# Transposes of batch 0's remainder and of half of batch 1 moved from TensorE to DMA, with new slots and a new order of loads

## The chip, the cores and the metric

One core of one Trainium2 chip. The metric is device microseconds of one execution; a kernel's figure is the median of several executions. Small comparisons are made as ratios: the mean time of one kernel's fast runs over that of the other's in the same rounds, with a 95% interval, so a ratio is not quite the quotient of the two medians quoted beside it.

Two more numbers are used. The profiled span is that of one traced execution. "The touched stretch" is, within one trace, the time from the first down-projection matmul (about 26 us) to the first up-projection matmul of the second token tile (83 us before).

## The reference

A retention layer (linear attention with decay) feeds a mixture of four experts, all of them applied to every token:

```python
# q, k, v: (8 batches, 8 heads, 576 positions, 64)
scores = q @ k^T / sqrt(64)
ret    = scores * gamma_h ** (i - j)   # i >= j, else 0
x      = (ret @ v), heads side by side           # (4608 tokens, 512)
out    = sum_e p[:, e] * (relu(x @ w1[e]) @ w2[e])   # w1: 512x1024, w2: 1024x512, e = 0..3
```

The kernel computes in bf16 with fp32 accumulation. It takes the tokens in nine tiles of 512; the attention of later batches is woven in between the expert matmuls of earlier tiles.

## The kernel before

The first tile is special: the weights are still on their way, and batch 1 is computed from four "units" (two halves of the sequence by two groups of heads), each with its own loads. The last 64 positions of a batch are its "remainder". Work is put into numbered slots: slot n is run after the n-th group of expert matmuls, and every engine executes its own part of the program in that order.

```python
# k and q have to be transposed before the scores. By TensorE, through PSUM and an ACT copy:
def trans_pe(self, between=0):                       # of a unit
    self.qk = atp.tile([128, 2, 2, 2, C], BF16, tag="qkT", name="qkT0")
    pt = ring_tile("pt", [128, 2, 2, 2, 2 * C], BF16)     # PSUM ring, 4 tiles
    for i, n in ((1, "k"), (0, "q")):
        ...
        nc.tensor.transpose(pt[:, i, r, g, 0:C], ..., ident)
    nc.scalar.activation(self.qk[...], pt[...], Copy)

# ... or by DMA:
def trans_dma(self):
    self.qk = atp.tile([128, 2, 2, 2, C], BF16, tag="qkT", name="qkT1")
    for i, n in ((1, "k"), (0, "q")):
        nc.sync.dma_start_transpose(out=self.qk[:, i]..., in_=self.bf(n)...)

# one group of an expert's up-projection (slots 0-3, 8-11, 16-19, 24-27)
def up_group(h, t, e, i):
    ph = ring_tile("ph", [128, 2, NT])
    ...                                              # 8 matmuls, 1.73 us
    if t == 0:
        nc.scalar.activation(h[:, fk:fk + 2, :], ph, Relu)   # frees the PSUM tile
        return

# loads, all in GpSimd's queue, in this order
load_w1(2); load_w2(2); load_v(0); load_v(1); load_w1(3); load_v(2); load_w2(3)   # load_v(3) later

def v_cast(u):
    vs[u].cast("k", nc.vector); vs[u].cast("q", nc.vector)
    vs[u].cast("v", nc.scalar)                       # ACT, in program order
    if u > 1:
        vs[u].trans_dma()                            # units 2 and 3 only
    if u == 0:
        load_v(3)

remainder(slots, 0, (-1, 13, 15, 16, 17))            # load, cast, transposes (TensorE), scores, values
for u, (c, tr, sc, o) in enumerate(((17, 20, 22, 23), (19, 22, 24, 25), (24, 0, 28, 29), (25, 0, 29, 30))):
    ...                                              # cast, transpose, scores and kv, values of unit u
```

So before, TensorE transposes the remainder of batch 0 and units 0 and 1; DMA transposes units 2 and 3, at a time when the loads are over.

Of the kernel before, what the change touches and what calls it, by code (L numbers as in the profile page):

```python
# [10 lines left out]
BF16 = mybir.dt.bfloat16  # L11
Copy = mybir.ActivationFunctionType.Copy
# [11 lines left out]
def kernel(  # L24
# [10 lines left out]
    nc = tc.nc  # L35
    B, H, S, D = q.shape
    N, E = moe_domain_probs.shape
# [3 lines left out]
    C = 128  # L41
    NC = 4
    SM = NC * C
    R = S - SM
    NP = H // 2
# [13 lines left out]
    atp = ctx.enter_context(tc.tile_pool(name="atp", bufs=2))  # L59
    ppool = ctx.enter_context(tc.tile_pool(name="ppool", bufs=4))  # L60
# [5 lines left out]
    def ring_tile(name, shape, dt=FP32):  # L66
        return ring.tile(shape, dt, tag="ring", name=name)
# [5 lines left out]
    def load_pair(t, b, p, eng=nc.sync):  # L73
        for n, src in srcs:
            for j in range(2):
                eng.dma_start(out=t[n][:, :, j, :],
                              in_=src[b, 2 * p + j, 0:SM, :].rearrange("(c p) d -> p c d", p=C))

    def load_rem(b, eng=nc.sync):
        for j in range(2):  # L80
            for n, src in (("k", k), ("v", v)):
                eng.dma_start(out=rawr[n][64 * j:64 * j + 64, :, j, :],
                                  in_=src[b, j:H:2, SM:S, :].rearrange("g t d -> t g d"))
        eng.dma_start(out=rawr["q"][0:R, :, :, :].rearrange("t g j d -> t (g j) d"),
                          in_=q[b, :, SM:S, :].rearrange("h t d -> t h d"))

    rawr = {n: const.tile([128, NP, 2, D], FP32, name=f"rawr_{n}") for n, _ in srcs}
    bfr = {n: const.tile([128, NP, 2, D], BF16, name=f"bfr_{n}") for n, _ in srcs}
    raw1 = {n: const.tile([128, NC, 2, D], FP32, name=f"raw1_{n}") for n, _ in srcs}
# [9 lines left out]
    def load_w1(e, f=slice(0, F)):  # L99
        return nc.gpsimd.dma_start(out=w1_sb[e][:, :, f], in_=moe_w1[e][:, f].rearrange("(dc p) f -> p dc f", p=128))  # L100

    def load_w2(e):
        return nc.gpsimd.dma_start(
            out=wx[e // 2][:, (e % 2) * NFC:(e % 2 + 1) * NFC, :, :].rearrange("p a b c -> p a (b c)"),
            in_=moe_w2[e].rearrange("(fc p) d -> p fc d", p=128))
# [9 lines left out]
    def load_unit(raw, b, hf, g, eng):  # L115
        for n, src in srcs:
            eng.dma_start(out=raw[n],
                          in_=src[b, 4 * g:4 * g + 4, 2 * C * hf:2 * C * hf + 2 * C, :]
                          .rearrange("h (p r) d -> p h (r d)", r=2))
# [21 lines left out]
    ident = const.tile([128, 128], BF16)  # L141
# [72 lines left out]
    pB = {}  # L214

    def load_p(t, e, eng):
        pB[t, e] = ppool.tile([128, NT], FP32, tag="pB", name="pB")
        eng.dma_start(out=pB[t, e], in_=pd[e:e + 1, t * NT:(t + 1) * NT].to_broadcast([128, NT]))  # L218
# [82 lines left out]
    class Rem:  # L301
# [12 lines left out]
            self.kT = atp.tile([128, NP, 128], BF16, tag="kTr", name="kTr", bufs=1)  # L314
            self.qT = atp.tile([128, NP, R], BF16, tag="qTr", name="qTr", bufs=1)

        def trans_pe(self):
            self.alloc_trans()
            pt = ring_tile("ptr", [128, 2, NP, 128], BF16)
            for i, n, w in ((0, "k", 128), (1, "q", R)):  # L320
                for p in range(NP):
                    nc.tensor.transpose(pt[:, i, p, 0:w], bfr[n][0:w, p, :, :].rearrange("p j d -> p (j d)"),
                                        ident[0:w, 0:w])
            nc.scalar.activation(self.kT, pt[:, 0], Copy)
            nc.scalar.activation(self.qT, pt[:, 1, :, 0:R], Copy)

        def trans_dma(self):
            self.alloc_trans()
            for dst, n, w in ((self.kT, "k", 128), (self.qT, "q", R)):
                nc.sync.dma_start_transpose(out=dst, in_=bfr[n][0:w, :, :, :].rearrange("p g j d -> p (g j d)"))  # L330
# [177 lines left out]
    class Unit:  # L508
# [29 lines left out]
                                 pt[:, :, :, :, 0:C].rearrange("p i r g t -> p i (r g) t"), Copy)  # L538

        def trans_dma(self):  # L540
            self.qk = atp.tile([128, 2, 2, 2, C], BF16, tag="qkT", name="qkT1")
            for i, n in ((1, "k"), (0, "q")):
                nc.sync.dma_start_transpose(out=self.qk[:, i].rearrange("p r g t -> p (r g) t"),
                                            in_=self.bf(n).rearrange("p r h d -> p (r h d)"))
# [152 lines left out]
    for g in range(2):  # L697
        kv1 = opool.tile([128, 2, 2, 4, D], BF16, tag="o", name=f"kv1_{g}")
        for n in "kqv":
# [7 lines left out]
    vs = [Unit(1, hf, g, {n: raws[2 * hf + g][n].rearrange("p (h r d) -> p h r d", h=4, r=2) for n in "kqv"},  # L707
               bf1[g], carry) for hf in range(2) for g in range(2)]

    def load_v(u):  # L710
        load_unit({n: raws[u][n].rearrange("p (h x) -> p h x", h=4) for n in "kqv"}, 1, vs[u].hf, vs[u].g, nc.gpsimd)
# [8 lines left out]
    load_w1(2)  # L720
    load_w2(2)
    load_v(0)
    load_v(1)
    load_w1(3)
    load_v(2)
    load_w2(3)

    def remainder(slots, b, at):
        add = lambda i, f: slots.setdefault(i, []).append(f)
        x = Rem(b)  # L730
        l, c, tr, s, o = at
        if b > 0:
            add(l, lambda: load_rem(b))
        add(c, lambda: x.cast(nc.vector))
        add(tr, x.trans_pe)
        add(s, x.scores)
        add(o, x.values)

    def run(slots, i):
        for f in slots.get(i, []):  # L740
# [2 lines left out]
    slots = {}  # L743
    add = lambda i, f: slots.setdefault(i, []).append(f)
    add(0, later_decays)
    add(3, mixing_weights0)
    add(9, mixing_weights)
    remainder(slots, 0, (-1, 13, 15, 16, 17))

    def v_cast(u):  # L750
        vs[u].cast("k", nc.vector)
        vs[u].cast("q", nc.vector)
        vs[u].cast("v", nc.scalar)
        if u > 1:
            vs[u].trans_dma()
        if u == 0:
            load_v(3)

    def v_head(u):
        vs[u].scores()  # L760
        vs[u].kv()

    for u, (c, tr, sc, o) in enumerate(((17, 20, 22, 23), (19, 22, 24, 25), (24, 0, 28, 29), (25, 0, 29, 30))):
        add(c, lambda u=u: v_cast(u))
        if u < 2:
            add(tr, lambda u=u: vs[u].trans_pe())
        add(o, lambda u=u: vs[u].values())
        add(sc, lambda u=u: v_head(u))
    add(26, lambda: [load_p(1, e, nc.sync) for e in range(E)])
    add(27, lambda: load_pair(raw1, 2, 0))  # L770
    add(27, lambda: load_rem(1))
    for j, ats in enumerate(((18, 18, 19, 20), (20, 21, 23, 23), (28, 28, 29, 29), (30, 30, 40, 41))):
        for at, which in zip(ats, (3, 1, 2, 4)):
            add(at, lambda which=which, j=j: w_sum(which, 4 * j, 4 * j + 4))
# [1 line left out]
    n = 0  # L776
# [18 lines left out]
    slots = {i - 32: f for i, f in slots.items() if i >= 32}  # L795
# [30 lines left out]
    for t in range(1, n_nt):  # L826
        d = [Down(h, t, s) for s in range(2)]
# [5 lines left out]
        n = NS * (t - 1)  # L833
# [40 lines left out]
```

## Time and profile before

| | before |
|---|---|
| median, 4 runs | 535.25 us (534.9 to 535.91) |
| profiled span | 533.5 us |
| TensorE busy | 526.2 us, 99% |
| the touched stretch | 57.6 us (25.68 to 83.30) |

The prediction below shows the lines that carry this. Read them with one question: which engine, if it were given less work, would let the kernel end sooner? In the stretch that the change touches it is TensorE. One thing to add is what ACT (ScalarE) does there: its timeline of before around unit 3's cast. Columns are start and duration in us, engine, line, operation and tiles; in brackets the idle time before it and what ended it.

```profile
68.47 1.02 ACT L361 ACTIVATE h<-ph 128x1024 bf16<-128x1024 f32 x1
69.39 0.76 ACT L637 ACTIVATE xt<-o 128x256 bf16<-128x256 f32 x2
69.99 0.62 ACT L520 ACTIVATE kv<-raw_v 128x512 bf16<-128x512 f32 x1
70.73 1.02 ACT L361 ACTIVATE h<-ph 128x1024 bf16<-128x1024 f32 x1
```

The third line is unit 3's v cast. It didn't wait: its data had landed at about 68.1. Right behind it stands a Relu that frees a PSUM tile for TensorE. If that cast waits, so does the Relu.

### The profile page before, as it was taken

The numbers are of one execution on the slowest core, as the hardware profiler recorded it, in microseconds if no ns is written. First come the engines' busy times: TensorE is split into PE (matmuls) and PEld (weight loads), VectorE is DVE, ScalarE is ACT, GpSimd is POOL, SyncE is SP. The second block draws the span as 40 slices with busy tenths as digits, with TensorE's granted clock in tenths as the row PEclk, the third lists the DMA queues.
The fourth block names the chain that finished last, engine by engine and source line by source line (L and its number), as shares of the span: only waits on it lengthen the run. The fifth ranks groups of instructions, "written<-read, shape, count | busy, mean of one in ns | idle before, by whom it ended". The sixth has DMA issues, their size and how long they took to land.

```text
span 533.5 us, 10230 instructions
## 1 busy us (share of the span) xinstructions
PE 526.2 (99%) x4260; PEld 342.0 (64%) x4260; DVE 361.4 (68%) x456; ACT 85.9 (16%) x175; POOL 146.8 (28%) x189
## 2 busy tenths in 40 slices
PE   8999999999999999999999999999999999999997
PEld 4644544478745985478646865587548844884486
DVE  5436768895577667697578767776765567557763
ACT  4723440012101111020101101100110000000010
POOL 5743104235235334235132514153000000000000
PEclk9999999999999999999999999999999999999999
DMA  9999947867778866736353666454010111110001
GB/s 241 198 217 245 244 122 191 166 154 163 150 166 155 176 142 148 153 83 162 108 135 94 144 139 114 104 118 126 20 41 25 56 39 41 41 41 20 1 24 56
DMA packets 144510, 63.55 MB, mean 119 GB/s; under 512 B 123728, under 2 KB 135264, under 8 KB 144464
## 3 DMA queue, kind: packets, MB, share of 16 engines
q1 hardware_dynamic: 134080, 43.42, 36.1%
q0 software_dynamic: 10240, 19.35, 16.2%
q8 instruction: 33, 0.54, 0.4%
q10 hardware_dynamic: 144, 0.13, 0.1%
q14 instruction: 13, 0.11, 0.1%
HBM read 53.56 MB, written 9.51 MB: 118 GB/s over the span
## 4 chain that ended last, share of the span: by engine, by line
PE 73%; ACT 2%; DVE 0%; issue 0%
PE ph L357 37%; PE pd L469 34%; ACT xt L290 2%; PE o L282 1%; PE o L277 1%; PE py L469 1%; DVE h L363 0%; PE or L342 0%; PE sr L336 0%; PE or L344 0%; DVE ob L497 0%
## 5 line engine op out<-in xcount | busy, mean ns | idle before, releaser
L357 PE MATMUL ph<-xt,w 128*128 128x512 bf16 x1136 | 250.9, 379 | 0.8 <-DVE h L363 0.2
L363 DVE SCALAR_TENSOR_TENSOR h<-ph,pB 128x1024 bf16<-128x1024 f32 x128 | 156.3, 1223 | 58.1 <-PE ph L357 57.2
L357 PEld LDWEIGHTS <-w 128*128 128x128 bf16 x1136 | 109.9, 98 | 127.9
L469 PEld LDWEIGHTS <-h 128*128 128x128 bf16 x1024 | 100.0, 98 | 13.4
L469 PEld LDWEIGHTS <-s 128*128 128x128 bf16 x768 | 75.0, 98 | 8.7
L469 PE MATMUL pd<-wx,h 128*128 128x256 bf16 x512 | 61.1, 273 | 0.2
L469 PE MATMUL pd<-wx,s 128*128 128x256 bf16 x512 | 61.1, 273 | 0.0
L218 POOL DMA_DIRECT2D pB<-pd x28 | 15.7, 562 | 151.7 <-DVE h L363 150.8
L504 POOL TENSOR_TENSOR ob<-v,p 128x256 f32<-128x256 f32 x15 | 11.8, 784 | 111.8 <-DVE v L501 83.8
L237 POOL TENSOR_TENSOR bf_k<-raw_k,gk 128x512 bf16<-128x512 f32 x24 | 26.1, 1088 | 36.6 <-DMA raw_k<-in_k_dram 23.2
L269 DVE TENSOR_TENSOR sT<-s,tri 128x1024 bf16<-128x1024 f32 x24 | 28.2, 1218 | 6.4 <-PE s L267 6.4
L290 ACT ACTIVATE xt<-o 128x768 bf16<-128x768 f32 (+6 forms) x24 | 13.0, 594 | 116.8 <-PE o L282 116.8
L469 PE MATMUL pd<-t4w,h 128*128 128x256 bf16 x256 | 30.6, 273 | 0.0
L442 DVE TENSOR_TENSOR s<-s,h 128x1024 bf16<-128x1024 bf16 x32 | 29.9, 973 | 0.0
L392 PE MATMUL po<-wx,h 128*128 128x512 bf16 x128 | 29.1, 379 | 0.0
L469 PE MATMUL pd<-t2w,s 128*128 128x256 bf16 x240 | 28.7, 273 | 0.0
L469 PE MATMUL pd<-t3w,h 128*128 128x256 bf16 x240 | 28.6, 273 | 0.0
L477 ACT ACTIVATE p<-pd 128x256 f32<-128x256 f32 x16 | 6.1, 383 | 138.8 <-PE pd L469 106.2
L237 POOL TENSOR_TENSOR bf_q<-raw_q,gq 128x512 bf16<-128x512 f32 x24 | 26.6, 1109 | 5.0 <-DMA rawr_v<-in_v_dram 2.1
L446 DVE TENSOR_TENSOR s<-h,s 128x1024 bf16<-128x1024 bf16 x32 | 26.4, 863 | 0.0
L440 DVE TENSOR_TENSOR s<-h 128x1024 bf16<-128x1024 bf16 x32 | 23.7, 779 | 0.0
L486 DVE TENSOR_TENSOR u<-pd,p 128x256 f32<-128x256 f32 x15 | 6.4, 424 | 22.4 <-PE pd L469 22.3
(160 smaller groups left out, 376.4 us busy)
## 6 DMA issues: line engine op xcount, KB each, us to landing
pB<-pd POOLq DMA_DIRECT2D x28, 256.0 KB, 3.6
raw_k<-in_k_dram SPq DMA_DIRECT2D x48, 128.0 KB, 2.6
raw_q<-in_q_dram SPq DMA_DIRECT2D x48, 128.0 KB, 2.9
raw_v<-in_v_dram SPq DMA_DIRECT2D x48, 128.0 KB, 3.3
wx<-in_moe_w_dram POOLq DMA_DIRECT2D x4, 1024.0 KB, 14.5
out_dram<-oa SPq DMA_DIRECT2D x16, 256.0 KB, 2.4
out_dram<-ob SPq DMA_DIRECT2D x15, 256.0 KB, 2.2
w<-in_moe_w_dram POOLq DMA_DIRECT2D x3, 1024.0 KB, 13.8
```

What stands on the lines that cost most here:

```text
L218: eng.dma_start(out=pB[t, e], in_=pd[e:e + 1, t * NT:(t + 1) * NT].to_broadcast([128, NT]))
L237: eng.tensor_tensor(bfs[p % 2][n], raw1[n], g[:, :, 2 * p:2 * p + 2].unsqueeze(3).to_broadcast([128, NC, 2, D]), op=MULT)
L269: nc.vector.tensor_tensor(sT[:, :, :, :].rearrange("p j c t -> p (j c) t"), s[:, :, :, :].rearrange("p j c t -> p (j c) t"), tri[:, :].uns ...
L290: nc.scalar.activation(xt_of(t)[:, self.ps, n0 + a - t * NT:n0 + z - t * NT], o[:, :, a:z], Copy)
L357: nc.tensor.matmul(ph[:, f, :], lhsT=w1_sb[e][:, dc, fc * 128:(fc + 1) * 128], rhs=x[:, dc, :], start=(dc == 0), stop=(dc == NDC - 1))
L363: nc.vector.scalar_tensor_tensor(h[:, fk:fk + 2, :], ph, 0.0, pB[t, e][:, :].unsqueeze(1).to_broadcast([128, 2, NT]), op0=MAX, op1=MULT)
L392: nc.tensor.matmul(po[:, g, :], lhsT=h[:, e * NFC + fc, ns * 128:(ns + 1) * 128], rhs=wx[e // 2][:, (e % 2) * NFC + fc, :, :].rearrange("p ...
L440: nc.vector.tensor_tensor(self.alloc("s1")[:, l], h[:, l, self.b], h[:, r, self.b], op=ADD)
L442: nc.vector.tensor_tensor(self.alloc("s2")[:, l], self.s1[:, l], h[:, l, self.a], op=SUB)
L446: nc.vector.tensor_tensor(self.alloc("s4")[:, l], h[:, r, self.a], self.s2[:, l], op=SUB)
L469: mm = nc.tensor.matmul(dst, lhsT=src[:, kk, tok], rhs=rhs(c), start=(start and c == 0), stop=(c == KH - 1), skip_group_check=True)
L504: nc.gpsimd.tensor_tensor(self.ob[:, HF:Dm], self.v, self.p5, op=ADD)
```

## The change

Intent: take the transposes of the remainder and of units 0 and 1 off TensorE, the engine that bounds the kernel, and let DMA do them; give them more slots between cast and scores, since a DMA takes longer to land; find two more buffers for the results; bring the last expert's first weights ahead of unit 1's data.

```diff
         def trans_dma(self):
-            self.qk = atp.tile([128, 2, 2, 2, C], BF16, tag="qkT", name="qkT1")
+            pool, tag = (atp, "qkT") if self.hf else (ppool, "pB")
+            self.qk = pool.tile([128, 2, 2, 2, C], BF16, tag=tag, name="qkT1")
@@
     load_v(0)
+    load_w1(3)
     load_v(1)
-    load_w1(3)
     load_v(2)
@@
-    remainder(slots, 0, (-1, 13, 15, 16, 17))
+    rem0 = Rem(0)
+    for at, f in ((11, lambda: rem0.cast(nc.vector)), (11, rem0.trans_dma), (20, rem0.scores), (21, rem0.values)):
+        add(at, f)
@@
-        if u > 1:
-            vs[u].trans_dma()
+        vs[u].trans_dma()
@@
-    for u, (c, tr, sc, o) in enumerate(((17, 20, 22, 23), (19, 22, 24, 25), (24, 0, 28, 29), (25, 0, 29, 30))):
+    for u, (c, sc, o) in enumerate(((18, 25, 26), (21, 26, 27), (24, 28, 29), (25, 29, 30))):
@@
-    add(26, lambda: [load_p(1, e, nc.sync) for e in range(E)])
-    add(27, lambda: load_pair(raw1, 2, 0))
-    add(27, lambda: load_rem(1))
+    add(29, lambda: [load_p(1, e, nc.sync) for e in range(E)])
+    add(28, lambda: load_pair(raw1, 2, 0))
+    add(29, lambda: load_rem(1))
```

(The removed transposing functions of TensorE are cut.)

More of the change, by code (lines that the diff above doesn't have):

```diff
@@ L315, in alloc_trans @@
             self.qT = atp.tile([128, NP, R], BF16, tag="qTr", name="qTr", bufs=1)
-        def trans_pe(self):
-            self.alloc_trans()
-            pt = ring_tile("ptr", [128, 2, NP, 128], BF16)
-            for i, n, w in ((0, "k", 128), (1, "q", R)):
-                for p in range(NP):
-                    nc.tensor.transpose(pt[:, i, p, 0:w], bfr[n][0:w, p, :, :].rearrange("p j d -> p (j d)"),
-                                        ident[0:w, 0:w])
-            nc.scalar.activation(self.kT, pt[:, 0], Copy)
-            nc.scalar.activation(self.qT, pt[:, 1, :, 0:R], Copy)
         def trans_dma(self):
@@ L722 @@
     load_v(0)
+    load_w1(3)
     load_v(1)
-    load_w1(3)
     load_v(2)
     load_w2(3)
-    def remainder(slots, b, at):
-        add = lambda i, f: slots.setdefault(i, []).append(f)
-        x = Rem(b)
-        l, c, tr, s, o = at
-        if b > 0:
-            add(l, lambda: load_rem(b))
-        add(c, lambda: x.cast(nc.vector))
-        add(tr, x.trans_pe)
-        add(s, x.scores)
-        add(o, x.values)
     def run(slots, i):
@@ L761, in v_head @@
         vs[u].kv()
-    for u, (c, tr, sc, o) in enumerate(((17, 20, 22, 23), (19, 22, 24, 25), (24, 0, 28, 29), (25, 0, 29, 30))):
+    for u, (c, sc, o) in enumerate(((18, 25, 26), (21, 26, 27), (24, 28, 29), (25, 29, 30))):
         add(c, lambda u=u: v_cast(u))
-        if u < 2:
-            add(tr, lambda u=u: vs[u].trans_pe())
         add(o, lambda u=u: vs[u].values())
         add(sc, lambda u=u: v_head(u))
-    add(26, lambda: [load_p(1, e, nc.sync) for e in range(E)])
-    add(27, lambda: load_pair(raw1, 2, 0))
-    add(27, lambda: load_rem(1))
+    add(29, lambda: [load_p(1, e, nc.sync) for e in range(E)])
+    add(28, lambda: load_pair(raw1, 2, 0))
+    add(29, lambda: load_rem(1))
     for j, ats in enumerate(((18, 18, 19, 20), (20, 21, 23, 23), (28, 28, 29, 29), (30, 30, 40, 41))):
```

## The prediction

> **What bounds the kernel now.** I read the page's busy table first, then the order of TensorE's work around the change, then TensorE's waits there, then the DMA.
>
> ```profile
> PE 526.2 (99%) x4260; PEld 342.0 (64%) x4260; DVE 361.4 (68%) x456; ACT 85.9 (16%) x175; POOL 146.8 (28%) x189
> PEclk9999999999999999999999999999999999999999
> ```
>
> TensorE has work 99% of the span at full granted clock. So a microsecond of TensorE work removed is a microsecond gained, and a microsecond in which it is made to wait is one lost; other engines count only if they make it wait.
>
> The touched stage is the second half of the first token tile (46 to 83 us). Its timeline on TensorE:
>
> ```profile
> 46.40 0.39 PE L322 MATMUL ptr<-ident,bfr_k 128*128 128x128 bf16 x4
> 46.72 0.29 PE L322 MATMUL ptr<-ident,bfr_q 64*128 64x64 bf16 x4
> 46.94 1.90 PE L357 MATMUL ph<-xt,w 128*128 128x512 bf16 x8
> ...
> 55.93 0.39 PE L535 MATMUL pt<-ident,bf_k 128*128 128x128 bf16 x4
> 56.15 0.39 PE L535 MATMUL pt<-ident,bf_q 128*128 128x128 bf16 x4
> 56.38 3.62 PE L392 MATMUL po<-wx,h 128*128 128x512 bf16 x16
> ```
>
> The transposes to be removed stand here; the start of the next row says how long each held the pipeline. In this stage TensorE waits 0.2 us in all.
>
> The data side is the opposite of idle. Until 67 us the DMA engines are full (busy share over 1.1) with weights and batch 1, all in one queue (q0, issued by GpSimd). Two looks at the queues, each one microsecond long, 41 to 42 us, where one HWDGE transfer (the mixing weights' write, 528 packets) crosses that stream, and 70 to 71 us, where a DMA transpose runs alone:
>
> ```profile
> q0 software_dynamic: 144, 0.17, 96.1%
> q1 hardware_dynamic: 143, 0.02, 24.2%
> ...
> q1 hardware_dynamic: 524, 0.13, 63.5%
> ```
>
> ```profile
> qkT<-kv SPq DMA_TRANSPOSE x2, 2.5
> qkT<-q SPq DMA_TRANSPOSE x2, 3.2
> pd<-pn SPq DMA_DIRECT2D x1, 72.0 KB, 9.4
> ```
>
> Columns: packets, MB, share of the 16 engines; then median us from issue to landing. Alone, a transpose of 128x512 bf16 is some 528 packets and lands 2.5 us after issue. In the full stream the other transfer of as many packets got one packet for one of q0's and took 9.4 us.
>
> **What the Trainium skill says.** "DMA: Bandwidth & Descriptors", section "Queues, rings and completion order": each DMA engine goes round-robin, packet by packet, over the rows that have work. The 143 against 144 packets agree. Same page, "Issuing engines are not separate DMA queues": a transfer started elsewhere still shares the same 16 engines. So transposes from SP will delay the weights; q0's fall from about 0.21 to 0.17 MB per us beside that write agrees. "TensorE: Matmul & The Clock Gate", "Part 4: PE-mode transpose", gives about 275 ns for a transpose in a kernel; the trace shows 219 ns each, overlapped, and only about 57 ns of pipeline each, so there is little to win. Same page, "HAM oscillation — how this bites in real kernels": TensorE gaps over some 3.4 us bring the half clock back. Nothing in this trace has such a gap; it matters to my downside.
>
> **The change part by part.**
>
> Removed from TensorE: the remainder's 8 transposes (46.40 to 46.94, 0.54 us), unit 0's 8 (55.93 to 56.38, 0.45) and unit 1's 8 (60.93 to 61.39, 0.46). Sum 1.45 us. The ACT copies that go with them (0.60 + 0.38 + 2 x 1.02 = 3.0 us) are not on the path: ACT is 16% busy.
>
> Added: six DMA transposes in SP's queue while q0 is full. One costs 528 packets at 63.5% of a microsecond per 524, so 0.64 us of all engines, or 0.019 us per packet and engine. (The write above costs q0 0.04 of 0.21 MB over about four us, 0.76 us for its 528 packets: the same size.) Five full ones and a half one are 5.5 x 0.64 = 3.5 us of extra work in a stream that had no gaps.
>
> Do they land in time? Each up- or down-group is 1.73 us (6.91 for four). Counting from 46.40 without the transposes: remainder scores at 55.0, unit 0's at 64.0, unit 1's at 67.2, the third group of the last expert's up-part done at 66.8.
>
> Remainder: its data land by about 38.1, VectorE casts idle-handed by 39, but SP's transposes queue behind the mixing-weights write (landed 44.9). Then 800 packets at 100 to 144 per us are 6 to 8 us: landed about 51, ahead of 55.0. No wait.
>
> Unit 0: its k was waited for until 49.6 before; plus about 0.9 us for the remainder's transposes, 50.5 to 52.3 for k, q, v. Casts done 52.1, transposes start about 53.5, one for one with the third expert's w1 and unit 1's loads (2 KB packets, 100 to 130 per us): 1056 packets, 8 to 9 us, landed about 62.5 to 63.5. Needed at 64.0: just in time.
>
> Unit 1: third-expert w1 (1 MB, 4.7 us: before, landed 43.66 + 14.9 = 58.6) now goes first, so w1 lands about 57 instead, in time for its use at 60.6. Unit 1's loads, which landed 52.3 to 53.9, land about 58 to 60; casts done about 60; transposes follow unit 0's, landed 69 to 70. Needed at 67.2: a wait of 2 to 3 us.
>
> Unit 3 (kept at its slot): GpSimd's issue rule visible in the waits is that a load waits for the eighth load before it; the new order still lets unit 3's loads be issued about 60, ahead of the queue's end. They landed at about 52.8 + 13.8 = 66.6 (k), 67.4 and 54.4 + 13.7 = 68.1 (v). With three units' worth of transposes in front (51 + 68 + 68 packets per engine x 0.019 = 3.5 us) v lands at 71.6. Its cast sits on ACT in program order behind unit 0's work, which now comes at 65 to 66 us; before, ACT reached that cast at 69.99, with 1.9 us to spare. Now ACT waits to 71.6, casts (0.62), then does the held-up Relu (1.02): 73.3. The fourth up-group needs that Relu's PSUM buffer (a ring of four) and would have begun at 68.5 (68.24, plus the 0.3 us of small gaps that before also shows). So TensorE stops for about 4.8 us, inside which unit 1's wait is hidden. I see nothing later that gives it back.
>
> The later loads for batch 2, its remainder and the second tile's weights sit a little later but behind the same SP queue; before, it was issuing without a break from 69 to 93 us, and a TensorE that is late needs them later. I count 0.
>
> Sum: 535.24 - 1.45 + 4.8 = 538.6. I shade it to 538.0, because the delay of unit 3's data rests on adding packet costs and may be partly absorbed.
>
> **The rivals.**
>
> 1. Full lead: all transposes land in time and the loads aren't slowed noticeably. For it: the larger leads look chosen for this, the remainder has 4 us to spare, each transpose alone is 2.5 us. Against: q0 is full and unit 3's margin was 1.9 us. Time 533.8, 0.3% faster.
> 2. The wait takes the removed work's place, as above: 536 to 540. If only unit 1's transposes (2 to 3 us) bite, about 536.5; if unit 3's loads do, 538.6.
> 3. It is worse: the packets of two more transposes (unit 2's, about 1.3 us) also get in front of unit 3's loads, the last w2 arrives late for its group at 70.7, and a stop of over 3.4 us drops the clock for a while (about 2 us more). Each speaks for 541 to 543. For it: unit 2's casts are due at about 63, before q0 ends; against: they queue behind unit 1's transposes in the same SP row.
> 4. The write of the mixing weights delays the remainder's transposes past 55.0, a wait of 1 to 4 us at its scores. Against: the packet rates above leave 4 us to spare; I give it a tenth.
>
> **Range and chances.** The best case is bounded by the 1.45 us removed (533.8, 0.3%); the likely waits give 536 to 540; the worst stack of rival 3 gives 543. 8 in 10: 533.7 to 541.8. 2% is 10.7 us either way. Faster by so much is out of reach (0.01). Slower by it needs about 12 us of waits, more than all late loads that I can find (0.04). Within 2%: 0.95.
>
> **What would show it.** Right: on TensorE's timeline no identity transposes between 46 and 62 us, no gap at the remainder's scores, and a gap of 3 to 6 us around 67 to 73 us, ended by unit 1's transposes or by ACT's Relu, before the last expert's fourth up-group; on ACT an idle stretch ended by the DMA of unit 3's v; transposes in the crowded stretch landing 6 to 11 us after issue instead of 2.5; q0 done at about 70 us instead of 67. The clock row stays at 9. Wrong: no gap on TensorE over 0.5 us before 83 us (then rival 1, and my cost of the packets is too high), or gaps at 55 us (rival 4), or a gap in the first groups of the second tile, which would mean that the moved loads of batch 2 matter after all.

## The result

| | before | after |
|---|---|---|
| median, 4 runs | 535.25 us | 542.78 us (542.02 to 543.89) |
| ratio | | 1.0141 (1.012 to 1.0162) |
| profiled span | 533.5 us | 541.3 us |
| TensorE's granted clock, mean | 1.00 | 0.993 |
| the touched stretch | 57.62 us | 65.15 us (25.93 to 91.08) |

The changed kernel is 1.4% slower, 7.5 us. All of it lies in the touched stretch, which is 7.53 us longer; from the second tile on the two traces run alike.

TensorE's timeline of the changed kernel, at the places that the prediction named (columns as above):

```profile
60.81 3.62 PE L347 MATMUL ph<-xt,w 128*128 128x512 bf16 x16
66.65 0.64 PE L549 MATMUL s<-qkT 64*64 64x128 bf16 x16 [2.23 <-DMA qkT<-bf_q]
67.23 1.15 PE L567 MATMUL kvp<-bf_v,bf_k 128*128 128x128 bf16 x8
68.31 2.66 PE L347 MATMUL ph<-xt,w 128*128 128x512 bf16 x8
...
75.00 0.42 PE L549 MATMUL s<-qkT 64*64 64x128 bf16 x16 [3.46 <-DMA qkT<-bf_q]
75.35 0.72 PE L567 MATMUL kvp<-bf_v,bf_k 128*128 128x128 bf16 x8
76.17 3.08 PE L347 MATMUL ph<-xt,w 128*128 128x512 bf16 x8
```

The transposes are gone, and two waits have come, 2.23 and 3.46 us, each for the DMA transpose of q (unit 0's, unit 1's). And some of the work after each wait is slow: eight up-matmuls take 2.66 and 3.08 us where before they took 1.89. The stretches of the same timeline with the granted clock (busy us by engine in the columns, TensorE's first; the clock is the third figure from the end, then DMA share and GB/s) say why:

```profile
66.65:68.30 1.65, 1.65 (x24) 1.09 (x24) 0.96 (x1) 0.00 (x0) 0.00 (x0) 0.50 1.22 201
70.90:71.54 0.64, 0.63 (x19) 0.37 (x18) 0.00 (x0) 0.00 (x0) 0.00 (x0) 1.00 1.31 313
79.20:80.00 0.80, 0.80 (x20) 0.63 (x20) 0.00 (x0) 0.70 (x1) 0.00 (x0) 0.50 1.02 231
```

After either wait TensorE is granted half its clock for 3.41 us: from 66.47 to 69.88, and from 76.71 to 80.12. The second time that begins 1.7 us after the wait has ended; unit 1's scores and kv, at 75.00 and 75.35, still run at full clock. In this trace the clock changes on a grid of 3.41 us, and the stretches of that grid just before are

```profile
63.06:66.47 3.41, 1.37 (x7) 0.40 (x5) 2.19 (x4) 2.34 (x3) 0.00 (x0) 1.00 1.25 190
...
69.88:73.29 3.41, 1.65 (x23) 0.66 (x21) 0.69 (x1) 0.00 (x0) 0.00 (x0) 1.00 1.26 188
73.29:76.70 3.41, 1.60 (x27) 1.11 (x28) 1.92 (x2) 2.23 (x5) 0.00 (x0) 1.00 1.06 155
```

The stretches in which TensorE stood idle for 2.04 us (3.41 - 1.37) and 1.81 us are followed by half clock; the one with 1.76 us is not. So the place of a wait on this grid counts, not only its length.

ACT after, against the four lines of before:

```profile
74.45 0.63 ACT L510 ACTIVATE kv<-raw_v 128x512 bf16<-128x512 f32 x1 [4.93 <-DMA raw_v<-in_v_dram]
75.10 1.02 ACT L351 ACTIVATE h<-ph 128x1024 bf16<-128x1024 f32 x1
```

Unit 3's v comes at 74.4 instead of 68.1, and ACT, which now reaches its cast earlier, waits 4.93 us for it. The Relu behind it ends at 76.1, and the up-group at 76.17 is the one that needs its PSUM tile. So two holds of TensorE end within a microsecond of each other: unit 1's transposes at 75.0, unit 3's loads through ACT at 76.1. The list of waits would show only the first.

The transposes of the changed kernel between 36 and 76 us (median us from issue to landing at the end of the line), and the two queues at 55 to 56, 56 to 57 and 65 to 66 us:

```profile
qkT<-bf_k SPq DMA_TRANSPOSE x2, 11.0
qkT<-bf_q SPq DMA_TRANSPOSE x2, 13.2
...
kTr<-bfr_k SPq DMA_TRANSPOSE x1, 10.8
qTr<-bfr_q SPq DMA_TRANSPOSE x1, 12.3
```

```profile
q0 software_dynamic: 107, 0.22, 112.7%
...
q0 software_dynamic: 100, 0.25, 96.6%
q1 hardware_dynamic: 72, 0.02, 11.7%
...
q0 software_dynamic: 158, 0.16, 94.8%
q1 hardware_dynamic: 158, 0.03, 29.1%
```

A transpose takes 11 to 13 us to land. Unit 0's k was issued at 52.44, yet no packet of q1 moves before 56.2: some 3.8 us pass before the first one gets in. Then the queues alternate one for one (158 to 158 in a microsecond, and still 16 to 14 in a tenth of it, 65.0 to 65.1).

### The profile page after: what moved, and what is told of

It is laid out like the page before. It is cut to its first block, busy times and chain, and to the rows that moved or that the text cites. A ratio compares the mean times of both kernels' runs of the same rounds, so it can differ in the third digit from the quotient of the medians.

```text
span 541.3 us, 10192 instructions
## 1 busy us (share of the span) xinstructions
PE 528.0 (98%) x4236; PEld 342.1 (63%) x4236; DVE 362.6 (67%) x456; ACT 83.2 (15%) x171; POOL 148.1 (27%) x189
## 4 chain that ended last, share of the span: by engine, by line
PE 72%; ACT 2%; DVE 0%; issue 0%
PE ph L347 36%; PE pd L459 33%; ACT xt L290 2%; PE o L282 1%; PE o L277 1%; PE py L459 1%; DVE h L353 0%; PE or L332 0%; PE or L334 0%; PE sr L326 0%; DVE ob L487 0%
## 5 line engine op out<-in xcount | busy, mean ns | idle before, releaser
L459 PEld LDWEIGHTS <-h 128*128 128x128 bf16 x1024 | 100.0, 98 | 13.3
L432 DVE TENSOR_TENSOR s<-s,h 128x1024 bf16<-128x1024 bf16 x32 | 31.2, 1015 | 0.0
L382 PEld LDWEIGHTS <-h 128*128 128x128 bf16 x128 | 12.1, 99 | 14.2 <-ACT h L351 0.9
## 6 DMA issues: line engine op xcount, KB each, us to landing
w<-in_moe_w_dram POOLq DMA_DIRECT2D x3, 1024.0 KB, 13.6
```

Of the source, the lines that this page charges most:

```text
L382: nc.tensor.matmul(po[:, g, :], lhsT=h[:, e * NFC + fc, ns * 128:(ns + 1) * 128], rhs=wx[e // 2][:, (e % 2) * NFC + fc, :, :].rearrange("p ...
L432: nc.vector.tensor_tensor(self.alloc("s2")[:, l], self.s1[:, l], h[:, l, self.a], op=SUB)
L459: mm = nc.tensor.matmul(dst, lhsT=src[:, kk, tok], rhs=rhs(c), start=(start and c == 0), stop=(c == KH - 1), skip_group_check=True)
```

## The experiments

The theory after the result had four parts: (a) DMA transposes issued into the full stream land late; (b) they also push the loads behind them back, so that unit 3's v holds ACT, a Relu and a PSUM tile; (c) the holds of (a) and (b) end together, so undoing one shows little; (d) TensorE pays again, at half clock, after a gap. The main rival was that moved slots, buffers and the order of loads cost by themselves. "Stretch" is the touched stretch of the run's trace: 57.6 us before, 65.15 us after.

### The same slots and loads, transposes back on TensorE

```diff
-(11, rem0.trans_dma), (20, rem0.scores)
+(19, rem0.trans_pe), (20, rem0.scores)
-        vs[u].trans_dma()
+        if u != 0 and u != 1:
+            vs[u].trans_dma()
+        # unit 0: add(24, trans_pe); unit 1: add(25, trans_pe), into the buffers of the change
```

> The changed kernel, its slots, its order of loads and its buffers, but remainder, unit 0 and unit 1 transposed by TensorE again (slots 19, 24, 25). Theory (the DMA transposes are what costs): TensorE's two waits are gone, the loads land as in the kernel before, and unit 3's cast, now 4 us earlier in ACT's order, may hold the last up-group by up to 1.5 us; 535 to 537. Rival (moved slots and the order of loads cost by themselves): 540 to 543.

Measured: 535.51 us, ratio 0.9988 (0.9964 to 1.0013), stretch 57.63 us. TensorE's longest wait between 60 and 84 us was 0.2 us. So slots, buffers and order of loads cost nothing as long as TensorE transposes: the main rival is out, and what costs is the transposing by DMA.

### Only the order of loads undone

```diff
-    load_w1(3)
     load_v(1)
+    load_w1(3)
     load_v(2)
```

> The changed kernel with only the order of loads undone: unit 1's data again ahead of the last expert's first weights. Theory (the transposes wait for one another in SP's row behind packets shared one for one; unit 1's are queued behind unit 0's in any case): unit 1's data land some 4 us earlier but its transposes do not; the last expert's weights come about 62.5 instead of 58.2, a wait of 1 to 2 us before unit 0's scores that lies inside the wait for unit 0's transposes. No change within 0.6 us: 542.3 to 543.4. Rival (the order of loads made unit 1 late): 539 to 541.

Measured: 543.22 us, ratio 1.0146 (1.0125 to 1.0168), stretch 65.44 us. As expected, no change. Unit 1's scores now waited 4.92 us and started at 74.58 instead of 75.00, although its data landed 5.6 us earlier (k at 53.57 instead of 59.17). Its transposes, issued 0.8 us earlier (k at 59.08 instead of 59.92), queue behind unit 0's in the same row.

### The transposes beside the old program, read by nobody

The kernel before, with the same six DMA transposes issued after the casts into spare buffers; TensorE still does its own.

```diff
+    def dummy(pairs):
+        t = ppool.tile([128, 8, C], BF16, tag="pB", name="spare")
+        for lo, hi, src in pairs:
+            nc.sync.dma_start_transpose(out=t[:, lo:hi, 0:src.shape[0]], in_=src)
 ...
         if u > 1:
             vs[u].trans_dma()
+        else:
+            dummy([(0, 4, k of unit u), (4, 8, q of unit u)])
-    remainder(slots, 0, (-1, 13, 15, 16, 17))
+    remainder(slots, 0, (-1, 11, 15, 16, 17));  add(11, dummy of the remainder's k and q)
```

> The kernel before, which transposes on TensorE, with the same six DMA transposes issued beside it into spare buffers that nobody reads (from the same casts, at 11, 17 and 19). No wait on a transpose can occur. Theory (two separate harms, late transposes and late loads): the loads are pushed back by 4 to 6 us all the same, ACT waits for unit 3's v, and TensorE stops once for 2 to 4 us and gets the half clock after it; 538 to 541. Rival (only the wait on the transposes' landing costs): 535.2 to 536.

Measured: 537.84 us, ratio 1.0043 (1.002 to 1.0066), stretch 59.76 us. Just under the range given, and clear of the rival in the trace. Nothing waits for a transpose here, but the waits between 60 and 80 us show part (b) alone:

```profile
ACT kv L520 <- DMA raw_v<-in_v_dram: 3.0, 1, 3.0
...
PE po L392 <- ACT h L361: 1.8, 2, 1.5
```

ACT waits 3.0 us for unit 3's v (before: none), and TensorE 1.8 us for ACT's Relu. The half clock that was expected after it did not come in the traced execution (the longest of these waits was 1.5 us). The pushed-back loads by themselves are worth 2.1 us of the stretch. This kernel has TensorE's transposes too, so those 2 us are not masked by anything saved.

### One hold taken away, then the other, then both

Unit 3's casts two slots later:

```diff
-(24, 28, 29), (25, 29, 30))
+(24, 28, 29), (27, 29, 30))
```

> The changed kernel with unit 3's casts moved from slot 25 to slot 27, so that neither ACT nor VectorE is held by unit 3's loads before the last up-groups. Theory (two holds end within a microsecond of one another: unit 1's transposes at 75.0, and the Relu behind unit 3's cast at 76.1): taking one away leaves the other, so at most 0.3 us is gained; 542.4 to 542.9, the wait for unit 1's transposes still about 3.5 us. Rival (unit 3's hold alone sets the restart): 539 to 540.

Measured: 542.31 us, ratio 1.0125 (1.0108 to 1.0142), stretch 65.33 us. ACT isn't held before the last up-groups any more, and the restart comes from unit 1's transposes as before, at 74.42 after a wait of 4.99 us (expected: 3.5). The clock has a share in "no gain": here half clock was granted from 73.34 to 80.16, so TensorE worked at it for 5.7 us after the restart instead of 3.4. An estimate from these two figures, half their difference, is that 1.2 us of gain was lost to that.

Unit 1 transposed by TensorE, unit 3's casts where the change has them:

```diff
+        if u != 1:
-        vs[u].trans_dma()
+            vs[u].trans_dma()
+        # unit 1: add(25, trans_pe)
```

> The changed kernel with unit 1 transposed by TensorE (slot 25), the remainder and unit 0 still by DMA. Theory (two holds, as in the run before): the wait for unit 1's transposes is gone, but the last up-group still waits for the Relu behind unit 3's cast; with 1056 packets fewer in the crowd unit 3's v lands 1 to 2 us earlier, so about 541 (540.3 to 541.8). Rival (unit 1's transposes alone set the restart): their 3.5 us and 1.6 us of half clock fall away and 0.5 us of transposes comes back, 538.2.

Measured: 540.74 us, ratio 1.0099 (1.0084 to 1.0114), stretch 62.89 us. Waits of TensorE between 60 and 84 us:

```profile
PE ph L347 <- ACT h L351: 2.6, 1, 2.6
PE s L550 <- DMA qkT<-bf_q: 1.9, 1, 1.9
```

The hidden hold is now in the open: an up-group waits 2.6 us for the Relu. With a unit's packets fewer in the stream, unit 3's v cast could start at 72.14 instead of 74.45.

Both at once:

> Both of the last two at once: unit 1 transposed by TensorE and unit 3's casts at slot 27. Theory (two holds): only now does the time fall, by the second wait and its half clock; the wait for unit 0's transposes (2.2 us) and the half clock after it (1.6 us) stay: 537.5 to 538.7. Rival (one of the two was the cause alone): the same time as whichever single undoing worked.

Measured: 537.93 us, ratio 1.0052 (1.0033 to 1.0071), stretch 60.81 us. One undoing gained nothing in the stretch (65.33 against 65.15), the other 2.3 us, both together 4.3. That is the sign of two holds that end together. TensorE's waits between 60 and 84 us, which leave the clock out, show it too: 5.7 us in the changed kernel, 6.4 and 4.6 with one undone, 2.5 with both. What stays is unit 0's wait, 2.52 us in this trace, and the slow clock after it. That slow clock isn't there in every execution: two of the four ran at a mean clock of 1.000 (537.34 and 537.54 us), the other two, the traced one among them, at 0.996 and 0.997 (538.32 and 539.74 us).

### TensorE kept busy through the waits

The changed kernel, with 9 and 14 throwaway matmuls in front of the two waits. They write into the score tile, which the real matmuls overwrite.

```diff
             s = ring_tile("s0", [128, 2, 2, 2, C])
+            for _ in range({0: 9, 1: 14}.get(2 * self.hf + self.g, 0) if self.b == 1 else 0):
+                nc.tensor.matmul(s[:, 0]..., lhsT=w1_sb[0][:, 0, 0:128], rhs=xt_of(0)[:, 0, :], start=True, stop=True)
```

> The changed kernel with 9 and 14 throwaway matmuls (216 ns apart, so 1.9 and 3.0 us) put in front of the two waits of TensorE, 2.2 and 3.5 us long, which end at the transposes of units 0 and 1. Theory: the waits stay, but the granted clock does not fall to 0.50 after them, which costs about 3.2 us in two stretches of 3.4 us; so 542.8 - 3.0 = about 539.7, clock 1.00. Rival (the slow stretches after the gaps come from late data, not from the clock): no change, 542.8, and the matmuls after the gaps are as slow as before.

Measured: 540.88 us, ratio 1.0093 (1.0069 to 1.0117), stretch 63.42 us, clock 0.999. Its TensorE timeline after the waits:

```profile
68.23 0.42 PE L552 MATMUL s<-qkT 64*64 64x128 bf16 x16 [1.31 <-DMA qkT<-bf_q]
68.58 0.72 PE L570 MATMUL kvp<-bf_v,bf_k 128*128 128x128 bf16 x8
69.23 1.90 PE L347 MATMUL ph<-xt,w 128*128 128x512 bf16 x8
...
75.30 0.42 PE L552 MATMUL s<-qkT 64*64 64x128 bf16 x16 [0.58 <-DMA qkT<-bf_q]
75.65 0.72 PE L570 MATMUL kvp<-bf_v,bf_k 128*128 128x128 bf16 x8
76.55 1.89 PE L347 MATMUL ph<-xt,w 128*128 128x512 bf16 x8 [0.18 <-ACT h L351]
```

The slow stretches are gone (1.90 and 1.89 us for eight matmuls), so part (d) holds. But the stretch shrank by 1.73 us, not by 3. The half clock after the first wait had cost nothing in the end: TensorE only reached the second wait sooner and stood there until 75.3, a time set by the DMA. Only the second slow stretch is on the path.

### The remainder alone

```diff
-        add(tr, x.trans_pe)
+        add(tr, x.trans_dma)
-    remainder(slots, 0, (-1, 13, 15, 16, 17))
+    remainder(slots, 0, (-1, 11, 11, 20, 21))
```

> The kernel before, with only the remainder of batch 0 transposed by DMA at the new slots (cast and transposes at 11, scores at 20, values at 21); everything else as before. Theory (the crowd of DMA packets costs by number of packets): 800 of the 2976 new packets, the loads of unit 3 come 1 to 2 us later, which their margin of 1.9 us just takes; the time falls by the 0.54 us of TensorE work to about 534.7. Rival (any transpose in the full stream stops TensorE): 536 to 537.

Measured: 535.49 us against 535.39, ratio 0.9992 (0.9975 to 1.0009), stretch 57.46 us: 0.16 us instead of 0.54. Small waits of TensorE (0.20 us for ACT's Relu at 55.4, 0.16 us at 75.6) ate the rest. ACT stood 1.4 us waiting for unit 0's v, which now landed at 52.9, with a Relu of slot 18 behind it. With unit 0's casts one slot later:

```diff
-enumerate(((17, 20, 22, 23),
+enumerate(((18, 20, 22, 23),
```

> The kernel before with the remainder alone transposed by DMA (cast and transposes at 11, scores 20, values 21), and unit 0's casts at slot 18 instead of 17, so that ACT does not hold a Relu behind unit 0's later v, which ate 0.4 us in the earlier run of this part. Theory: the whole 0.54 us is gained now, 534.9 against 535.4 of before (ratio 0.999, hardly clear of noise), and in the trace the stretch from the first down-group to the second tile is 57.1 us instead of 57.6. Rival (a DMA transpose in the crowd always gives its gain back): no change in that stretch.

Measured: median 534.63 us against 535.18, stretch 57.21 us; but one of its six runs (539.76) and one of before's eleven (539.39) fell out, and the ratio is 0.9999 (0.9961 to 1.0038). So it was run again, unchanged:

> The version with the remainder alone by DMA once more, unchanged, because one of its six runs and one of before's fell out by 5 us and spoilt the interval. Theory (0.4 to 0.55 us gained): ratio 0.9988 to 0.9995, median 0.3 to 0.6 us under that of before. Rival (nothing gained): medians within 0.2 us.

Measured: 535.24 us against 535.32, ratio 0.9993 (0.998 to 1.0007). In this trace the touched stretch is 57.08 us, the full 0.54 us less, and yet the span is 533.6 us. The gain is given back two tiles later:

```profile
172.48 0.28 PE L336 MATMUL sr<-qTr,kTr 128*128 128x64 bf16 x4 [0.55 <-DMA qTr<-bfr_q]
```

The scores of a later remainder, whose transposes were DMA's already before, now come 0.55 us before their data. TensorE's lead is only part of the reason: these transposes took 5.2 us to land here and 4.1 us in the trace of before. The trace of the run with unit 0's casts at slot 17 has the same wait (0.46 us at 173.20), the first trace of the present program doesn't. So the gain of this part is shown in the touched stretch, and not shown in the kernel's time.

### Unit 0 earlier

The remainder and unit 0 by DMA, unit 1 by TensorE at slot 24, unit 3's casts at slot 27, and unit 0's loads ahead of the third expert's second weights, its casts at slot 16 (unit 1's loads go ahead of the last expert's first weights again):

```diff
-    load_w2(2); load_v(0); load_w1(3); load_v(1); load_v(2)
+    load_v(0); load_w2(2); load_v(1); load_w1(3); load_v(2)
-enumerate(((18, 25, 26), (21, 26, 27), (24, 28, 29), (25, 29, 30)))
+enumerate(((16, 25, 26), (21, 26, 27), (24, 28, 29), (27, 29, 30)))
```

> The remainder and unit 0 by DMA, unit 1 by TensorE, unit 3's casts at slot 27, and unit 0's loads ahead of the third expert's second weights, its casts at slot 16: its transposes are issued some 4 us earlier. Theory (unit 0's transposes are late because they are issued late into the crowd): landed by about 61 to 62, no wait at unit 0's scores (needed about 64), no half clock; what is left is the removal of 1.0 us: about 534.4 to 535.2, if the third expert's second weights, now later, still come by 53.5. Rival (the crowd delays them to 66 whenever they are issued): 537.5 to 538.5 as with both undone.

Measured: 535.23 us against 535.18, ratio 1.0003 (0.9975 to 1.0032; an outlier on either side, 538.38 and 539.39, widens it), stretch 57.83 us. Unit 0's transposes were issued at 48.53 and 49.81 instead of 52.44 and 53.72; the second took 14.6 us and landed at 64.4, not at the 61 to 62 expected, and just early enough. No wait there, no half clock. New small waits took what was gained: 0.8 us at 74.18 for unit 2's transposes, and, in the second tile, 0.7 us for those of batch 1's remainder:

```profile
94.63 0.28 PE L326 MATMUL sr<-qTr,kTr 128*128 128x64 bf16 x4 [0.71 <-DMA qTr<-bfr_q]
```

The next expectation misreads both: it takes the 0.7 us for a wait of batch 0's remainder (whose transposes landed at 51.1, its scores began at 54.92 without a wait) and the 0.8 us for unit 3's. So its edit, the scores and values of batch 0's remainder one slot later, moves something that was not late:

```diff
-(20, rem0.scores), (21, rem0.values)
+(21, rem0.scores), (22, rem0.values)
```

> The version with unit 0's loads first, and now the remainder's scores and values one slot later (21 and 22), since its transposes came 0.7 us too late there. Theory (each piece of lead that covers the landing turns into its 0.5 us): the 0.7 us wait goes, the 0.8 us wait at unit 3's scores stays; 534.4 to 534.9. Rival (the wait only moves to a later place): 535.2 as before.

Measured: 535.61 us against 535.32, ratio 1.0002 (0.9989 to 1.0014). The touched stretch is the shortest of all, 56.78 us, 0.84 less than before, since in this trace unit 2's transposes landed at 71.8 and not at 74.0 and nothing waits for them; that the edit did this isn't shown. But in the second tile stands

```profile
94.10 0.28 PE L326 MATMUL sr<-qTr,kTr 128*128 128x64 bf16 x4 [1.20 <-DMA qTr<-bfr_q]
```

a wait of 1.20 us for the transposes of batch 1's remainder, which before had a margin of about a microsecond. It is the wait of 0.71 us again, at the same place; so the run speaks neither for the theory nor for the rival (the wait moves to a later place). TensorE's lead is not the whole of it either: the transpose of q was issued at 91.66 here and at 90.34 before, and took 2.3 us in both. This version, like the changed kernel, has batch 2's and that remainder's loads in later slots.

No version beats the kernel before beyond noise.

## Why the prediction was right or wrong

**What bounds the kernel, and the 1.45 us removed:** right. In the second trace with the remainder alone the stretch falls by the 0.54 us counted for it; the 0.91 us of units 0 and 1 were not measured alone.

**The sign and the chain of events:** right, but for one wait that it did not have: 2.23 us for unit 0's transposes, which it called just in time. Unit 1's transposes are waited for, unit 3's v holds ACT, the Relu holds a PSUM tile of the last up-group, and one wait hides the other; the four runs that undo one hold, the other, both, or make only the loads late show it. The remainder was in time, as the prediction had it. Slots and the order of loads were counted as free, and within noise they are. Of the signs it named, three failed with the size: transposes landed 10.8 to 13.6 us after issue (6 to 11 named), q0's last packets moved between 73 and 74 (about 70), and the clock did not stay at 9.

**The step that failed is the size of the stop, "about 4.8 us".** The prediction had the held-up Relu done at 73.3; it was done at 76.1, and the up-group began at 76.17. Taking off the 0.25 us by which this trace began late, that is 2.6 us more: in the prediction's terms, from 68.5 on, a stop of 7.4 us. Half clock after it adds about 1.7 us, the measured loss of stretch that throwaway matmuls took back; the prediction named it in rival 3 for stops over 3.4 us and left it out of a sum whose own stop was 4.8. 3.35 us (its sum of 538.6 less 535.24), 2.6, 1.7 and 0.25 make 7.9; the spans differ by 7.8. The shading down to 538.0 went the wrong way.

**Inside the 2.6 us, the terms that were mis-sized:**

- When unit 0's transposes get in. "Transposes start about 53.5" fits a lone transpose, which needs 1.3 us from issue to its first packet (69.00 to 70.28 before). In the crowd it took 3.8 us (52.44 to 56.2). The view of before held this already: the mixing weights' write was issued at 35.5 and its first packets moved at 39. Unit 0 landed at 66.5 instead of 62.5 to 63.5 (53.5 and its "8 to 9 us" make 61.5 to 62.5, so its own sum was a microsecond off; the packets took 10.3 us).
- Unit 1 queues behind it: scores at 75.0 instead of data at 69 to 70.
- The delay of unit 3's v: 6.3 us (68.1 to 74.4) where 3.5 was summed. The prediction left unit 2's transposes out of that sum, "about 1.3 us", in rival 3. Nearly half of their packets were in front: from 56 to 74.4 q1 moved 2,590, of which units 0 and 1 make 2,112. The rest, some 2 us by subtraction, has no experiment of its own. The trace has two moments in which the engines moved next to nothing although they are booked as busy: the two queues of the changed kernel at 44 to 45 and at 72 to 73 us are

```profile
q0 software_dynamic: 60, 0.06, 80.2%
q1 hardware_dynamic: 65, 0.01, 59.6%
...
q1 hardware_dynamic: 162, 0.04, 91.2%
q0 software_dynamic: 9, 0.02, 26.8%
```

against 150 and 150 packets in an ordinary microsecond of the crowd. What stops them is open.

**"I count 0" for the later loads:** true for the changed kernel, whose TensorE was late too. For the versions that gained, it was wrong: the remainders of later batches had so little margin that 0.5 to 1.2 us of waiting came back there, in part because TensorE came earlier and in part because their transposes landed later.

**Rivals:** the truth was rival 2's mechanism with two of rival 3's additions, the half clock and, in part, unit 2's packets; no wait for a late w2 shows. The range's upper end, 541.8, was 1.0 us too low, since it gave the additions of rival 3 too little weight. Within 2%, at 0.95, held.

## What to carry to other kernels

Work taken off the bounding engine and given to DMA is not free if the DMA stream it joins is already full: count when the first packet gets in, how many packets it then shares turns with, and what the loads behind it hold up, down to the engine that executes their casts in program order. When undoing one wait gains nothing, look for a second one that ends at the same time before giving up the theory. And a gain of half a microsecond on the bounding engine can be lost again at any later transfer that has less margin than that. Before moving anything to cure a wait, read from the timeline at what time it stands: a list of waits names a line, and here one line served the remainders of all batches.

## What the Trainium skill lacked or had wrong

- "TensorE: Matmul & The Clock Gate", "HAM oscillation — how this bites in real kernels": its rule is no TensorE gap over some 3.4 us. Here gaps of 2.23, 2.52 and 2.62 us were followed by a granted clock of 0.50; gaps of 1.45, 1.94 and 1.98 us were not. The rule lacks how much idling within one window is enough: on the grid of 3.41 us on which the clock changed, after the first 24 us of each trace, TensorE had been idle for 1.81 to 3.41 us of the stretch before half clock set in (six times in five traces), and for at most 1.76 us in the seven other full-clock stretches with over a microsecond of idling.
- "DMA: Bandwidth & Descriptors", "Specifications": first-byte latency of the HWDGE path about 0.6 us. In a full stream the first packet of a transpose came 3.8 us after issue (52.44 to 56.2; 3.7 to 3.9 us in the seven traces that have unit 0's), against 1.2 to 1.3 us for a lone one, and no page tells how this latency grows with load.
- Same page, "Queues, rings and completion order": turns of whole packets of some 9 to 17 descriptors. In the records of this profile the turns are single ones, 158 to 158 per microsecond and 16 to 14 in a tenth of one, of 256 bytes against 1 KB (0.03 to 0.16 MB), so the row with small packets gets a small share of the bytes. Whether a record is a packet in the page's sense isn't shown, and the page doesn't draw that conclusion for transposes.
- Same page, "DMA Transpose (X-bar)": no figure for a transpose in a crowd. 128x512 bf16 made some 528 packets, 2.5 us alone and 11 to 14 us here. Nor does a page mention the moments in which all queues nearly stop (0.07 MB in a microsecond).
- "TensorE: Matmul & The Clock Gate", "Part 4: PE-mode transpose": about 275 ns per transpose; here 219 ns, overlapped to 57 ns of pipeline each.
